# Two ReLUs to VectorE, two weight casts to GpSimd, and a tighter schedule for batch 1 in a fused FFT filter and FFN kernel

## The chip, the cores and the metric

The kernel runs on one core of one Trainium2 chip. The metric is the device time of one execution in microseconds (us). Seven runs of the kernel before gave a median of 795.35 us, from 794.17 to 797.23 us. Besides these, one execution was taken with the hardware profiler; all durations below come from it.

## The reference

The input `x` has 8 batches of 3008 rows with 256 columns. Each batch goes through a filter in the frequency domain along its rows, and all 24064 resulting rows go through a two-layer network with a squared ReLU:

```
X = np.fft.rfft(x, axis=1)
y = np.fft.irfft(X * (filt_r + 1j * filt_i)[None], n=3008, axis=1)
h = np.maximum(y.reshape(24064, 256) @ w_in, 0.0)     # w_in: 256 x 2048
out = h * h @ w_out                                   # w_out: 2048 x 256
```

## The kernel before, in words

**The filter of one batch** is done with matrix products in four stages, because 3008 = 64 x 47. Stage A (`unit_a`, L346) transforms along the 47; its result `u` goes to a scratch tensor `dU` in device memory and is read back in another order as `ut` (`read_u`, L430). Stage B (`unit_b`, L437, twelve units p = 0 to 11) transforms along the 64 into PSUM (`psB`); VectorE multiplies with the filter (L451), makes two half copies (L458, L459) and adds (`unit_s`, L465). Stage P (`unit_p`, L487, twelve units) transforms back into `psP`; ScalarE evacuates it (L496) and every third unit writes to the scratch tensor `dZ` (L499). `read_z` (L508) reads `dZ` back as `zt` (eight DMAs on the SP queue), and stage Y (`unit_y`, L516, sixteen units n = 0 to 15) finishes into `yt`, evacuated by ScalarE for even n (and for n = 12 to 15 of batch 0) and by VectorE for the other odd n (L537, L539).

**The network** runs over 47 groups of 512 rows, each in 8 slots. In slot k of group g, `ffn_g1` (L544) computes two blocks of 128 hidden units into the PSUM tile `psH` (four matmuls of 512 columns, L560) and ScalarE applies the ReLU and writes float16 `h` (L564). `ffn_sq` (L566) squares it on VectorE (L568). One group later `ffn_g2` (L570) multiplies with `w_out` into `psO` (eight matmuls of 256 columns, L577), and `ffn_out` (L580) evacuates `psO` on ScalarE and stores. The first half of a product sums over the `h` of slots 0 to 3 and of the weight rows of cast chunks 0 and 1, the second half over the rest.

**The order is written out by hand**; every engine works off its instructions in the order in which the program issues them. Global slot s issues, in this order: `ffn_g1`; the filter work planned for (s, place 0); `ffn_g2` of the group before; the filter work of (s, place 1); `ffn_out`; `ffn_sq`. `fft_plan(b)` (L608) gives the slots of batch b's filter work. For batch 1, plan slot r is global slot r. So on VectorE the square of slot s stands behind all filter work of slot s. Batch 0's filter is done in a prologue before slot 0, except for its stage Y units 4 to 15, which are planned into slots 4 to 23.

**Buffers** that matter here are rings of two: `psH` (so the product of slot s waits for the ReLU of slot s-2), and `psF`, which stages A, B, P and Y share in order of issue (a unit waits until the tile of two units before is evacuated). `h` has two buffers too; the second group's takes the place of the float32 `w_out` that the four `cast_wout` (L329, 1024 columns each) turn into float16 `sWout`. In slots 0 to 7 there is no `psO` work yet, and slot 8's `psH` needs the four stage Y units of slots 4 to 7.

Of the kernel before, what the change touches and what calls it, by code (L numbers as in the profile page):

```python
# [11 lines left out]
AF = mybir.ActivationFunctionType  # L12
# [98 lines left out]
def kernel(  # L111
# [9 lines left out]
    nc = tc.nc  # L121
# [38 lines left out]
    def psO(name):  # L160
        return pps.tile([128, 2, 256], F32, tag="psO", name=name, bufs=2)

    def psH(name):
        return pps.tile([128, 2, 512], F32, tag="psH", name=name, bufs=2)
# [107 lines left out]
    ps = psO("warm").rearrange("p a d -> p (a d)")  # L272
# [267 lines left out]


    h2s, pso = {}, {}

    def ffn_g1(g, s):  # L544
        if s == 0:
            h2s[g] = p_h2.tile([128, NJT, TG], F16, tag="h2", name=f"h2_{g}")
        h2 = h2s[g]
        ps = psH(f"psH_{g}_{s}")
        segs = []
        t = g * TG  # L550
        while t < (g + 1) * TG:
            b, r = divmod(t, S)
            n = min((g + 1) * TG - t, S - r)
            segs.append((t - g * TG, b, r, n))
            t += n
        for i in range(2):
            jt = 2 * s + i
            for o, b, r, n in segs:
                for dt in range(2):
                    nc.tensor.matmul(ps[:, i, o:o + n],  # L560
                                     sWin[:, dt, jt * 128:(jt + 1) * 128],
                                     yts[b][:, dt, r:r + n],
                                     start=(dt == 0), stop=(dt == 1))
        nc.scalar.activation(out=h2[:, 2 * s:2 * s + 2, :], in_=ps, func=AF.Relu)  # L564

    def ffn_sq(g, s):  # L566
        v = h2s[g][:, 2 * s:2 * s + 2, :]
# [40 lines left out]
    def fft_plan(b):  # L608

        plan = {}  # L610

        def put(r, place, f, *a):
            plan.setdefault((r, place), []).append((f, a))

        if b == 1:
            for n in range(4, 16):
                put(n if n < 8 else n + 2 if n < 12 else 2 * n - 7, n % 2, unit_y, 0, n)
            for k in range(4):
                put((4, 5, 7, 7)[k], 1, cast_wout, k, nc.vector)
        t0 = 2 if b == 1 else 6  # L620
        for a in range(12 if b == 1 else 0, 16):
            put(t0 + a // 2, a % 2, unit_a, b, a)
        put(10 if b == 1 else 14, 1, read_u, b)
        t0 = 14 if b == 1 else 18
        for p in range(12):
            r = t0 + (18 if b == 1 else 19) * p // 11
            put(r, 0, unit_b, b, p)
            put(r, 0, unit_s, b, p)
            put(r + 2, 1, unit_p, b, p)
        t0 = 35 if b == 1 else 40  # L630
        for c in range(4):
            put(t0, 1, read_z, b, c)
        if b + 1 < B:
            for c in range(2):
                put(t0 - 13, 1, load_x, b + 1, c)
            for c in range(4):
                r = t0 - 8 + 3 * c
                put(r, 1, cast_x, b + 1, c)
                if c < 2:
                    put(r, 1, load_x, b + 1, c + 2)  # L640
        for n in range(16):
            if b == 1:
                put(38 + n // 2 if n > 3 else 39, n % 2, unit_y, b, n)
            else:
                put(44 + n // 2, n % 2, unit_y, b, n)
        return plan
# [79 lines left out]
    for b in range(1, B):  # L726
        first = (b * S // TG) * SLOTS - (48 if b > 1 else 40)
        for (r, place), w in fft_plan(b).items():
            work[(first + r, place)] = w

    for s in range((NG + 1) * SLOTS):
        g, k = divmod(s, SLOTS)
        if g < NG:
            ffn_g1(g, k)
        run(work, s, 0)
        if g > 0:
            ffn_g2(g - 1, k)
        run(work, s, 1)
        if g > 0:
            ffn_out(g - 1, k)  # L740
        if g < NG:
            ffn_sq(g, k)
# [30 lines left out]
```

## Time and profile before

| what | value |
|---|---|
| median of seven runs | 795.35 us |
| profiled execution, device time | 797.66 us |
| its span, first to last instruction | 795.8 us |
| granted TensorE clock, mean | 0.997 |
| busy: PE / VectorE (DVE) / ScalarE (ACT) / GpSimd (POOL) | 781.6 / 552.5 / 554.9 / 24.3 us |
| GpSimd's last instruction ends | 43.94 us |
| slot 0's first `psH` matmul starts | 51.65 us |
| slot 8's `psO` matmuls start | 62.81 us |
| VectorE busy, 80 to 100 us and 100 to 120 us | 18.95 and 19.32 us |

The profile page gives the busy time of each engine. The chain of waits follows the last instruction back to what released it, step by step. The timeline lists each engine's instructions with start, duration, source line and, in square brackets, the idle time before it and what ended that. A matmul's printed duration includes its way through the array; four of 512 columns show 1.03 us from the first start to the last end, but the next matmul can start 0.86 us after the first start.

### The profile page before, as it was taken

How to read it: one execution, taken by the hardware profiler on the slowest of the kernel's cores; microseconds unless marked ns; L12 is line 12 of the kernel's file. 1: busy time of each engine (PE TensorE's matmuls, PEld its weight loads, DVE VectorE, ACT ScalarE, POOL GpSimd, SP SyncE). 2: the span in 40 equal slices, each digit the busy share in tenths (PEclk: the TensorE clock that was granted, in tenths of full speed). 3: DMA queues.
4: the chain of work that ended last, by engine and by line, in shares of the span. 5: the costliest groups of instructions: out<-in, count | busy, mean ns of one | idle time of the engine just before them, and what ended most of it. 6: DMA issues, size and time to landing. Idle time of an engine off the chain costs nothing.

```text
span 795.8 us, 14801 instructions
## 1 busy us (share of the span) xinstructions
PE 781.6 (98%) x6102; PEld 553.2 (70%) x6102; DVE 552.5 (69%) x898; ACT 554.9 (70%) x708; POOL 24.3 (3%) x27
## 2 busy tenths in 40 slices
PE   8989999999999999999999999999999999999998
PEld 6746767666676676867777676776767667776666
DVE  6946995579755897559965699557995589554342
ACT  3856776777677677767777677676777767766664
POOL 3710000000000000000000000000000000000000
PEclk9999999999999999999999999999999999999999
DMA  9994555346723567055471555525664342511111
GB/s 352 358 274 140 143 149 133 88 134 163 198 57 107 161 163 180 31 166 151 123 180 51 168 153 136 130 70 156 151 182 89 89 140 80 137 35 41 40 41 54
DMA packets 88139, 107.32 MB, mean 135 GB/s; under 512 B 6288, under 2 KB 78864, under 8 KB 83856
## 3 DMA queue, kind: packets, MB, share of 16 engines
q1 hardware_dynamic: 87864, 106.19, 46.8%
q8 instruction: 48, 0.79, 0.4%
q10 hardware_dynamic: 144, 0.18, 0.1%
q14 instruction: 19, 0.16, 0.1%
q0 software_dynamic: 64, 0.00, 0.0%
HBM read 58.12 MB, written 48.23 MB: 134 GB/s over the span
## 4 chain that ended last, share of the span: by engine, by line
PE 91%; DMA 5%; DVE 2%; ACT 1%; issue 0%; SPq 0%; POOL 0%; ACTq 0%; POOLq 0%
PE psO L577 40%; PE psH L560 38%; PE psA L359 3%; PE psY L530 3%; PE psB L443 2%; PE psP L494 2%; DMA ut<-dU 2%; DMA zt<-dZ 1%; DMA xw<-in_x_dram 1%; PE warm L274 1%; DVE ut L428 1%; ACT h L564 1%; DMA dU<-u 0%; DMA dZ<-ze 0%; PE psf L293 0%; DVE h L568 0%
## 5 line engine op out<-in xcount | busy, mean ns | idle before, releaser
L564 ACT ACTIVATE h<-psH 128x1024 f16<-128x1024 f32 x376 | 385.2, 1025 | 190.6 <-PE psH L560 187.7
L577 PE MATMUL psO<-sWout,h 128*128 128x256 f16 x3008 | 388.7, 272 | 0.0
L560 PE MATMUL psH<-yt,sWin 128*128 128x512 f16 (+7 forms) x1728 | 386.9, 351 | 1.8 <-DVE yt L539 0.8
L577 PEld LDWEIGHTS <-h 128*128 128x128 f16 x3008 | 290.6, 98 | 77.3
L568 DVE TENSOR_TENSOR h<-h 128x1024 f16<-128x1024 f16 x376 | 253.8, 685 | 100.7 <-ACT h L564 99.2
L560 PEld LDWEIGHTS <-sWin 128*128 128x128 f16 x1728 | 159.5, 98 | 101.7 <-issue 3.5
L451 DVE TENSOR_TENSOR prod<-psB,sF 128x1024 f16<-128x1024 f32 x84 | 102.4, 1219 | 6.7 <-PE psB L443 6.5
L539 DVE CAST yt<-psY 128x376 f16<-128x376 f32 x62 | 34.0, 549 | 57.4 <-PE psY L530 57.4
L365 DVE CAST u<-psA 96x512 f16<-96x512 f32 x50 | 34.3, 687 | 47.3 <-PE psA L359 45.1
L496 ACT CAST ze<-psP 128x512 f16<-128x512 f32 x84 | 49.2, 586 | 17.8 <-PE psP L494 15.9
L588 ACT COPY ost<-psO 128x512 f32<-128x512 f32 (+1 forms) x96 | 55.7, 580 | 6.7 <-PE psO L577 5.3
L530 PEld LDWEIGHTS <-zt 112*128 112x128 f16 x512 | 34.9, 98 | 12.0 <-issue 1.6
L530 PE MATMUL psY<-sC,zt 112*128 112x94 f16 x512 | 42.3, 205 | 0.7 <-DMA zt<-dZ 0.4
L465 DVE TENSOR_TENSOR yf<-prod,yf 128x512 f16<-128x512 f16 x84 | 35.7, 425 | 2.9
L443 PE MATMUL psB<-ut,sSB 128*128 128x256 f16 x192 | 36.5, 272 | 1.0 <-DMA ut<-dU 0.8
L359 PE MATMUL psA<-x,sC 94*96 94x512 f16 x96 | 36.6, 382 | 0.0
L443 PEld LDWEIGHTS <-sSB 128*128 128x128 f16 x192 | 18.6, 98 | 21.8 <-issue 2.7
L494 PE MATMUL psP<-yf,sSP 128*128 128x256 f16 x168 | 32.1, 273 | 0.2 <-ACT yt L537 0.2
L537 ACT CAST yt<-psY 128x376 f16<-128x376 f32 x66 | 30.7, 468 | 1.1 <-PE psY L530 0.6
L338 DVE CAST x<-x 94x2048 f16<-94x2048 f32 x24 | 29.2, 1216 | 0.0
L363 ACT CAST u<-psA 96x512 f16<-96x512 f32 x50 | 28.6, 572 | 0.0
L458 DVE COPY yf<-prod 64x512 f16<-64x512 f16 x84 | 24.3, 289 | 2.9
(63 smaller groups left out, 253.2 us busy)
## 6 DMA issues: line engine op xcount, KB each, us to landing
x<-in_x_dram SPq DMA_DIRECT2D x20, 768.0 KB
zt<-dZ SPq DMA_DIRECT2D x64, 192.0 KB
dU<-u SPq DMA_DIRECT2D x28, 384.0 KB
dZ<-ze SPq DMA_DIRECT2D x28, 384.0 KB
out_dram<-ost SPq DMA_DIRECT2D x66, 128.0 KB
out_dram<-ost SPq DMA_DIRECT2D x31, 256.0 KB
ut<-dU SPq DMA_DIRECT2D x7, 1024.0 KB
xw<-in_x_dram SPq DMA_DIRECT2D x4, 1024.0 KB
```

Of the source, the lines that this page charges most:

```text
L359: nc.tensor.matmul(ps[0:96, :], sSA, x16s[(b, c)][:, m, :], start=True, stop=True)
L443: nc.tensor.matmul(ps[:, i * D:(i + 1) * D], sSB[:, 2 * p + i, :], uts[b][:, 2 * p + i, :], start=True, stop=True)
L451: nc.vector.tensor_mul(out=prod, in0=ps.rearrange("p (a d) -> p a d", d=D).unsqueeze(1).to_broadcast([128, 2, 2, D]), in1=sF[:, :, 2 * p:2 ...
L465: nc.vector.tensor_add(out=yf, in0=prod[:, 0], in1=yf)
L494: nc.tensor.matmul(ps[:, i * D:(i + 1) * D], sSP[:, 2 * p + i, :], yf[:, i, :], start=True, stop=True)
L496: nc.scalar.copy(out=zes[(b, c)][:, 2 * i6:2 * i6 + 2, :], in_=ps.rearrange("p (a d) -> p a d", d=D))
L530: nc.tensor.matmul(ps[:, 94 * jj:94 * jj + 94], zt[:, 4 * (g % 2) + jj, dt * 128:(dt + 1) * 128], sSY, start=True, stop=True)
L560: nc.tensor.matmul(ps[:, i, o:o + n], sWin[:, dt, jt * 128:(jt + 1) * 128], yts[b][:, dt, r:r + n], start=(dt == 0), stop=(dt == 1))
L564: nc.scalar.activation(out=h2[:, 2 * s:2 * s + 2, :], in_=ps, func=AF.Relu)
L568: nc.vector.tensor_mul(out=v, in0=v, in1=v)
L577: nc.tensor.matmul(pso[g][:, t % 2, :], h2s[g][:, jt, t * 128:(t + 1) * 128], sWout[:, jt, :], start=(jt == 0), stop=(jt == NJT - 1))
L588: nc.scalar.copy(out=ost[:, h0:h0 + step, :], in_=pso[g][:, h0:h0 + step, :])
```

## The change

Three edits, all of which concern slots 0 to 39, that is the first network groups and batch 1's filter.

1. The ReLUs of slots 2 and 5 of group 0 are done by `nc.vector.tensor_relu` instead of ScalarE's activation.
2. Of the four casts of `w_out`, chunks 0 and 1 go from VectorE to GpSimd (slots 4 and 5 as before). Chunks 2 and 3 stay on VectorE; chunk 2 is issued in slot 6 instead of slot 7, so ahead of slot 7's stage Y unit 7.
3. In batch 1's plan the twelve units of stage B spread over 17 slots instead of 18, and stage P follows two slots later as before; `read_z` goes from slot 35 to 34, the loads of batch 2's `x` from 22 to 21, and its casts from slots 27, 30, 33, 36 to 26, 29, 32, 35 (with the loads that follow the first two).

Unit p of stage B is in these slots:

| p | 0 | 1 | 2 | 3 | 4 | 5 | 6 | 7 | 8 | 9 | 10 | 11 |
|---|---|---|---|---|---|---|---|---|---|---|---|---|
| before | 14 | 15 | 17 | 18 | 20 | 22 | 23 | 25 | 27 | 28 | 30 | 32 |
| after | 14 | 15 | 17 | 18 | 20 | 21 | 23 | 24 | 26 | 27 | 29 | 31 |

```diff
+    on_vector = {(0, 2), (0, 5)}
...
-        nc.scalar.activation(out=h2[:, 2 * s:2 * s + 2, :], in_=ps, func=AF.Relu)
+        if (g, s) in on_vector:
+            nc.vector.tensor_relu(out=h2[:, 2 * s:2 * s + 2, :], in_=ps)
+        else:
+            nc.scalar.activation(out=h2[:, 2 * s:2 * s + 2, :], in_=ps, func=AF.Relu)
...
             for k in range(4):
-                put((4, 5, 7, 7)[k], 1, cast_wout, k, nc.vector)
+                put((4, 5, 6, 7)[k], 1, cast_wout, k, nc.gpsimd if k < 2 else nc.vector)
...
         for p in range(12):
-            r = t0 + (18 if b == 1 else 19) * p // 11
+            r = t0 + (17 if b == 1 else 19) * p // 11
             put(r, 0, unit_b, b, p)
             put(r, 0, unit_s, b, p)
             put(r + 2, 1, unit_p, b, p)
-        t0 = 35 if b == 1 else 40
+        t0 = 34 if b == 1 else 40
```

## The prediction

> **What bounds the kernel now.** I read the page first: it says which engine is full.
>
> ```profile
> PE 781.6 (98%) x6102; PEld 553.2 (70%) x6102; DVE 552.5 (69%) x898; ACT 554.9 (70%) x708; POOL 24.3 (3%) x27
> ```
>
> PE is busy for 98% of the span, and from slot 8 on its matmuls follow each other without a gap for most of the time. So an edit counts only by what it does to PE's gaps. The chain of waits from 50 to 64 us shows the gaps of the first group (start, duration, engine and line):
>
> ```profile
> 52.94 1.03 ACT h L564
> 53.97 0.04 issue
> 54.02 1.04 PE psH L560 x4
> 55.05 0.02 issue
> 55.08 1.95 ACT h L564 x2
> 57.02 0.02 issue
> 57.05 0.69 DVE h L568
> 57.74 0.61 DVE sWout L331
> 58.34 0.61 DVE h L568
> 58.96 0.46 DVE yt L539
> 59.42 0.60 DVE sWout L331
> 60.02 1.20 DVE h L568 x2
> 61.22 0.47 DVE yt L539
> 61.69 0.04 issue
> 61.73 0.81 PE psH L560 x3
> ```
>
> Up to 57.02 ScalarE's ReLUs set the pace, and from 57.05 VectorE does, without a pause, until its evacuation of stage Y unit 7 lets slot 8's second matmul start at 61.73. How much is there to win? Between 54.02 and 62.38 (PE's next other work) PE issues seven `psH` of 0.86 and four stage Y units of 0.17, 6.70 of 8.36 us: 1.66 us of gaps. The same view from 62.5 to 125 us is PE, but for some 0.3 us near 82.5, and then about 0.75 us at slots 39 and 40, where the first stage Y units of batch 1 wait for each other's evacuation.
>
> **ReLUs and casts in the first group.** I walk VectorE's queue with the durations of the chain. The price of a ReLU on VectorE is not in the trace; the nearest rows (mean ns of one after the bar) have its shape, or its size out of SBUF:
>
> ```profile
> L428 DVE CAST ut<-psT 128x1024 f16<-128x1024 f32 x2 | 2.4, 1218 | 1.1 <-PE psT L420 1.1
> L331 DVE CAST sWout<-wout 128x1024 f16<-128x1024 f32 x4 | 2.7, 684 | 0.0
> ```
>
> I take d = 1.22, since the source is PSUM; 0.68 is the low end, and the slowest VectorE row of 1024 columns (L451, 1.219 mean) says that 1.23 is the high end. ScalarE's is 1.02.
>
> - Slot 2: VectorE has the square of slot 1 at 54.91 and is free 0.60 later, at 55.51, although the product is ready at 55.06. ReLU 55.51 to 56.73; on ScalarE it ended at 56.05. The new wait is PE's: slot 4's product waits for this ReLU in the `psH` ring, so it starts at 56.78, not 56.15, and all PE work stands behind it.
> - Slot 4: product ready 1.02 later, at 57.80; ScalarE's ReLU 57.84 to 58.86; square on VectorE at 58.89.
> - Slot 5: ReLU behind that square, 59.50 to 60.72. Slot 7's product waits for it: 60.77 instead of 59.58, a PE gap of 0.83.
> - VectorE goes on: stage Y unit 5 at 60.64 (0.47), square 5 at 61.11 (0.60), cast 2, now here, at 61.71 (0.61), square 6 at 62.32 (0.61), unit 7 at 62.93. Plus 0.47 and 0.04: slot 8's second matmul starts at 63.44 instead of 61.73.
>
> So the two casts that leave save 1.21, but two ReLUs and the earlier cast 2 put 2 x 1.14 + 0.61 in, and the ring wait adds the rest: **+1.71 us**. With d left open, unit 7 starts at 60.49 + 2d against 61.22 before: +0.65 at d = 0.68, and no loss only below 0.36. PE then is gapless, so nothing gives the time back.
>
> Casts 0 and 1 on GpSimd I cost at nothing. GpSimd is empty after 43.94, so nothing is queued behind them. The data were there at 57.74, when VectorE's cast started unheld. GpSimd's casts of 1024 columns take 1.02 to 1.56; two end by 60.9 at the latest, and `psO` of slot 8 needs them at 62.81, or 64.5 in the new order. That cover is 1.9 us; beyond it each late us is a PE us. The low end is 0; the high end is VectorE held by GpSimd's use of the memory, bounded by what one such meeting cost in this row, 1.56 less 1.02, twice: 1.1. I take 0.
>
> ```profile
> 12.06 1.56 POOL L232 CAST xw<-xw 128x1024 f16<-128x1024 f32 x1 [9.39 <-DMA xw<-in_x_dram]
> ```
>
> This row ran beside a VectorE cast (12.03, 0.69, no longer than the others of its kind); later ones took 1.02. It was GpSimd that paid. The Trainium skill, "GPSIMD Engine Reference" (its opening table), speaks against edit 2: GpSimd shares its SBUF interfaces with VectorE, and two-port or two-input VectorE instructions contend; it does not say who pays. By that rule alone the sum could be 1.1 higher, by the row it stays.
>
> **Stages B and P closer together.** "Moved up" is a squeeze: units 0 to 4 stay, units 5 and 7 to 11 come one slot earlier, unit 6 stays; P likewise. VectorE is the tight engine there: 18.95 and 19.32 of 20 us busy. Durations from the timeline, start to start: unit B 2.22 (1.26 + 0.30 + 0.32 + 0.34), square 0.60, cast of x 1.14; a PE slot is 1.73, plus 0.22 for each B or P and 0.17 for a Y. I walk with times as before, without the shift above:
>
> - Up to slot 20 nothing changes; VectorE starts unit 4 (B4) at 88.31. Then: square 20, unit 5 at 91.13, squares 21 and 22, unit 6 at 94.57 (before: 95.21).
> - Slot 23 now holds B6, Y15 and P5. P5 wants the `psF` tile of B6, whose multiply ends at 95.79; PE would be there at 95.40. PE waits **0.43**, with slot 24 behind it.
> - Square 23, B7 97.39, squares 24 and 25 to 100.83, B8 101.23, x cast, square 26, B9, squares 27 and 28, B10 at 108.63, x cast, squares 29 and 30 to 113.21. Now B11 comes in slot 31, ahead of square 31; before it came after it, in slot 32. B11 113.21 to 115.43, square 31 until 116.12.
> - Slot 33's `psO` reads slot 31's `h` with its last two of eight matmuls, 0.65 after its start, that is at 115.38 with the 0.43 included. They wait **0.78**.
>
> The last wait had little slack before (timeline; slots 30 and 31's squares, slot 33's `psO`, B11):
>
> ```profile
> 113.28 1.28 DVE L568 TENSOR_TENSOR h<-h 128x1024 f16<-128x1024 f16 x2
> 114.30 1.04 PE L577 MATMUL psO<-sWout,h 128*128 128x256 f16 x8
> 114.49 1.21 DVE L451 TENSOR_TENSOR prod<-psB,sF 128x1024 f16<-128x1024 f32 x1
> ```
>
> The squares ended at 114.56, needed at 114.95: 0.39 of slack, against 2.22 of B11 put in front, less what comes from the earlier start. Together **+1.21**, from -0.75 (if slots 39 and 40 lost their gap) to +2.2 (a whole unit B). Behind the waiting P5 stand slot 24's `psH` and B7, for which ScalarE and VectorE wait; behind slot 33's `psO` stand P11, its `dZ` write and the `zt` reads.
>
> The DMAs that move are on SP: `dZ` writes, eight `zt` reads, four x loads and, with their odd slots unmoved, the output stores they pass. SP waits in this stage for evacuations (11.9 us for `ze`, 11.7 for the x casts), so order costs nothing there. The `zt` reads were issued from 118.42 to 124.07, and stage Y at 124.94 did not wait for them: to have them earlier gains nothing. An x cast held by a late load would hold square 32 or 35, needed at slots 40 and 41: 8 us and more of cover. GpSimd's queue has nothing else to pass.
>
> **Sum.** 1.71 + 1.21 = 2.92 us on the profiled execution: 797.66 to 800.6, span 798.7. The median stands 2.31 lower than that execution, so I forecast 795.35 + 2.9 = **798.3**, its own range 797.5 to 799.2.
>
> **Rivals.**
> 1. Only the first group costs (19%): VectorE catches up and P5 waits on nothing. 795.35 + 1.7 = 797.1. For it: VectorE idled 0.38 and 0.21 us at 92.39 and 102.55. Against: the 2.22 in front of square 31.
> 2. The faster side (6%): the ReLUs fit into VectorE's idle time and relieve ScalarE, whose ReLUs hold the `psH` ring up to 57. Price: at most the 1.66 us of gaps, 793.7. It decides from d below 0.36; no row of that size is under 0.68.
> 3. TensorE's clock drops (13%). Rows by stretch:
>
> ```profile
> 40.00:43.00 3.00, 0.52 (x4) 0.25 (x3) 0.00 (x0) 1.01 (x1) 1.09 (x2) 1.00 1.01 309
> 44.00:47.00 3.00, 3.00 (x9) 1.41 (x8) 1.38 (x2) 0.48 (x1) 0.00 (x0) 0.50 0.47 134
> ```
>
> PE was busy 0.52 of 3 us, and from 44 to 47 the granted clock was 0.50. In my walk PE works 1.25 of the 3.5 us before 63.44 (gaps 0.83 and 1.43). If that trips it, some 3.3 us at half speed cost 1.7: 800.0. The Trainium skill, "TensorE: Matmul & The Clock Gate" (Part 1), puts the drop after an idle window of about 3.4 us; by that rule my gaps are too short and the sum has no such term.
>
> 4. The change does not act as named (12%): the ReLU runs at the 0.68 end and the squeeze is hidden: 795.35 + 0.65 = 796.0.
>
> **How the numbers follow.** The forecast has 50%. Slower by over 0.2% (1.6 us, about what a measurement tells from no change, so above 796.94): forecast, rival 3 and 0.12 of rival 1: 0.75. Within: rival 4 and 0.07 of rival 1: 0.19. Faster: 0.06. The range reaches from rival 4 (795.9) to rival 3 with a little of the upper bounds (800.6).
>
> **What would show it.** Right: a VectorE row for the ReLU near 1.22 us; PE waiting for VectorE's `h` at slots 4 and 7; slot 8's second matmul near 63.4; P5 waiting for `prod`; slot 33's `psO` waiting for the square. Wrong: a ReLU under 0.7 us, or slot 8 before 61.73; PE gapless from slot 20 to 34; gaps gone at slots 39 and 40.

## The result and the profile after

The changed kernel takes 800.2 us, the median of 16 runs (798.27 to 802.12), against 796.08 us, the median of 40 runs of the kernel before (the seven shown above and later ones). The ratio is 1.0052, with a 95% interval from 1.0042 to 1.0062: slower by 4.1 us, between 3.3 and 4.9. The forecast was slower, by 2.9 us. The profiled execution took 799.73 us; its span is 798.0 us, 2.2 us longer than that of the profiled execution before.

The page's line of busy times hardly moves, because busy time does not show waits:

```profile
PE 780.3 (98%) x6102; PEld 552.5 (69%) x6102; DVE 554.7 (70%) x898; ACT 553.4 (69%) x706; POOL 26.8 (3%) x29
```

In the changed file the VectorE ReLU is line 566, ScalarE's 568 and the square 572; `psH` is 561 and `psO` 581. This is the chain of waits of the first group after the change (start, duration, engine and line), to be laid beside the one from 52.94 us in the prediction:

```profile
51.54 2.83 DVE h L572 x2
54.37 1.15 DVE h L566
55.52 0.04 issue
55.56 1.04 PE psH L561 x4
...
57.68 0.69 DVE h L572
58.37 1.14 DVE h L566
...
60.56 0.60 DVE sWout L331
61.16 0.60 DVE h L572
61.76 0.47 DVE yt L539
62.23 0.04 issue
62.27 0.81 PE psH L561 x3
```

The chain has become VectorE's. Both ReLUs (L566) stand on it, then cast 2 and square 6, and slot 8 waits for the evacuation (L539) as before. But the first line was not in the prediction: the squares of slots 0 and 1 take 2.83 us together, where one took 0.69. At that time GpSimd does its two casts (timelines of GpSimd and VectorE, one instruction a line):

```profile
51.35 1.04 POOL L331 CAST sWout<-wout 128x1024 f16<-128x1024 f32 x1 [8.20 <-DMA wout<-in_moe_w_out_dram]
51.54 1.39 DVE L572 TENSOR_TENSOR h<-h 128x1024 f16<-128x1024 f16 x1 [2.00 <-DMA zt<-dZ]
52.33 1.50 POOL L331 CAST sWout<-wout 128x1024 f16<-128x1024 f32 x1
52.85 1.52 DVE L572 TENSOR_TENSOR h<-h 128x1024 f16<-128x1024 f16 x1
```

The bracket of the first square names a DMA that ended about then; the ReLU that this square needs ended at 51.5 too. The rows look like taking turns: the first cast starts ahead of a square and keeps its usual 1.04 us, and each instruction that starts while the other engine's is under way takes 0.5 to 0.8 us longer. The casts are written in slots 4 and 5, but GpSimd has nothing else in its queue, so they start when `w_out` has landed, at 51.35, beside the squares of slots 0 and 1.

Further on, PE's timeline shows the two waits of stages B and P (in brackets the wait and what ended it):

```profile
96.48 0.38 PE L494 MATMUL psP<-yf,sSP 128*128 128x256 f16 x2 [0.27 <-DVE prod L451]
116.78 0.39 PE L581 MATMUL psO<-sWout,h 128*128 128x256 f16 x2 [0.59 <-DVE h L572]
```

The bracket counts from the modelled end of the matmul before, which overlaps the next; by starts the two waits are 0.43 and 0.75 us.

**Where the 2.2 us of the two spans lie.** I cut the span at first `psH` matmuls; these lengths are used below. G runs from slot 0's first `psH` matmul to slot 8's second, M from slot 14 to slot 35.

| stretch | before | after | difference |
|---|---|---|---|
| start to slot 0 | 51.65 | 49.20 | -2.45 |
| G, slot 0 to slot 8 | 10.08 | 13.07 | +2.99 |
| slot 8 to 14 | 12.63 | 12.63 | 0 |
| M, slot 14 to 35 | 42.76 | 44.07 | +1.31 |
| slot 35 to 41 | 12.55 | 12.54 | -0.01 |
| slot 41 to the end | 666.13 | 666.49 | +0.36 |

G and M together are +4.3, close to the 4.1 of the medians. The -2.45 is not the change's doing, since the change touches nothing ahead of slot 0: in this execution of the kernel before, PE waited 2.48 us for GpSimd's cast of x and the clock was at 0.50 from 44 to 47 us; in this one of the changed kernel it waited 1.73 us and the clock stayed at 1.00. That recurs below.

### The profile page after: what moved, and what is told of

The parts are those of the page before. It is cut to its first block, busy times and chain, and to the rows that moved or that the text cites. A ratio compares the mean times of both kernels' runs of the same rounds, so it can differ in the third digit from the quotient of the medians.

```text
span 798.0 us, 14800 instructions
## 1 busy us (share of the span) xinstructions
PE 780.3 (98%) x6102; PEld 552.5 (69%) x6102; DVE 554.7 (70%) x898; ACT 553.4 (69%) x706; POOL 26.8 (3%) x29
## 4 chain that ended last, share of the span: by engine, by line
PE 89%; DMA 5%; DVE 4%; ACT 1%; issue 0%; SPq 0%; POOL 0%; ACTq 0%; POOLq 0%
PE psO L581 38%; PE psH L561 37%; PE psA L359 3%; PE psY L530 3%; PE psB L443 2%; PE psP L494 2%; DMA ut<-dU 2%; DMA zt<-dZ 1%; DVE h L572 1%; DVE prod L451 1%; PE warm L274 1%; DMA xw<-in_x_dram 1%; PE psf L293 1%; PE psf L296 1%; ACT sF L303 0%; DMA dU<-u 0%
## 5 line engine op out<-in xcount | busy, mean ns | idle before, releaser
L539 DVE CAST yt<-psY 128x376 f16<-128x376 f32 x62 | 34.0, 549 | 58.0 <-PE psY L530 58.0
```

## The experiments

Times are differences of medians to runs of the kernel before on the same chip. The ratio beside them is not that of the two medians, so it can say up to 0.9 us more or less; its 95% interval decides what is a difference.

**One edit at a time.** First edit 1 alone (the diff's first part), then edit 2 alone, edit 3 alone, and edits 1 and 2 together.

> Edit 1 alone: the ReLUs of slots 2 and 5 on VectorE, all four casts on VectorE in slots 4, 5, 7, 7, no squeeze. Two stage lengths tell the theories apart: G, from slot 0's first psH matmul to slot 8's second (10.08 us in the kernel before, 13.07 in the changed one), and M, from slot 14's first psH matmul to slot 35's (42.76 before, 44.07 changed). My theory has three separate prices: the ReLUs behind squares in VectorE's queue (+1.7), squares held by GpSimd's casts in front of the first ReLU (+1.3), the squeeze (+1.2 to 1.3). It expects the squares of slots 0 and 1 to take 0.69 us each, G 11.8, M 42.8, time +1.7 us. Rival: the slow squares come from DMA traffic that lands in the same microseconds, not from GpSimd: squares near 1.4 us here too, G 13.1, time +3.0.

> Edit 2 alone: casts 0 and 1 on GpSimd, cast 2 on VectorE in slot 6. My theory: the squares of slots 0 and 1 are held by GpSimd's casts and take about 2.8 us together where they took 1.4, but with the ReLUs on ScalarE no product waits for VectorE there, and the queue has caught up by slot 5; cast 2 in slot 6 stands ahead of stage Y unit 7. G 10.2, M 42.8, time +0.1 us (no difference that can be measured). Rival, that the casts on GpSimd are what costs by themselves: G 11.4, time +1.3. Rival, that DMA traffic slows the squares: squares as in the kernel before, 0.69 us each, or slow in the run with edit 1 alone too.

> Edit 3 alone: stages B and P of batch 1 over 17 slots, reads of dZ and the x loads and casts one slot earlier. My theory: G 10.08 as before; P5 waits 0.43 for the multiply of B6, slot 33's last two psO matmuls wait 0.75 for the square of slot 31; M 44.0, time +1.2 us. Rival: the waits of this stage in the changed kernel are carried over from the late first group, and the squeeze alone costs nothing: M 42.8, time as before.

> Edits 1 and 2 without the squeeze. My theory: the price of the ReLUs and that of the held squares meet, since slot 2's ReLU now stands behind the held squares: G 13.1, M 42.8, time +3.0 us. Rival, that the two edits only add up (edit 1 +1.7, edit 2 near nothing): G 11.8, time +1.7.

| run | time | ratio, interval | G | M |
|---|---|---|---|---|
| edit 1 alone | +2.0 | 1.0030 (1.0013 to 1.0047) | 11.85 | 42.77 |
| edit 2 alone | -0.4 | 1.0004 (0.9987 to 1.0020) | 10.32 | 42.81 |
| edit 3 alone | +1.5 | 1.0022 (1.0008 to 1.0037) | 10.08 | 43.96 |
| edits 1 and 2 | +1.7 | 1.0026 (1.0010 to 1.0042) | 12.57 | 42.77 |

Edit 1 alone, VectorE's timeline around slot 2's ReLU:

```profile
55.19 0.69 DVE L572 TENSOR_TENSOR h<-h 128x1024 f16<-128x1024 f16 x1 [2.00 <-ACT h L568]
56.10 0.69 DVE L572 TENSOR_TENSOR h<-h 128x1024 f16<-128x1024 f16 x1 [0.22 <-ACT h L568]
56.71 1.22 DVE L566 TENSOR_SCALAR h<-psH 128x1024 f16<-128x1024 f32 x1
```

The squares take 0.69 us, the ReLU 1.22 and follows the square: G grows by 1.77, with GpSimd out of it. The walk gave 1.71 for edits 1 and 2 together; it holds here too, since cast 0 falls into VectorE's idle time ahead of square 4 and cast 1 stands where the walk has cast 2. Edit 3 alone has both its waits and M +1.20, without the late first group: nothing is carried over.

Edit 2 alone was not what I expected in one respect: its squares were at 0.69 us. In that execution slot 0 began at 52.70 and GpSimd's casts ran from 52.35 to 54.38, before the first square at 55.05; they did not meet. In the run with edits 1 and 2 slot 0 began at 49.22, the casts ran from 50.86 to 53.34 and the squares from 51.57, at 2.32 together: they met, and G is 0.72 longer than with edit 1 alone. In the changed kernel they met more, and it is 1.22 longer. The expectation for edits 1 and 2 (G 13.1, time +3.0) was too high; the time, +1.7, is what its rival had, and G, 12.57, is between the two. So the third price depends on when slot 0 starts against a transfer that lands at its own time.

**Does GpSimd hold VectorE, and which instructions?** One run lets GpSimd start behind slot 1's square, with edits 1 and 2:

```
     def ffn_sq(g, s):
...
+        if (g, s) == (0, 1):
+            nc.gpsimd.tensor_copy(out=gate, in_=h2s[0][0:1, 3, 511:512])
```

> Edits 1 and 2 as in the run before, but GpSimd first copies one element of slot 1's square, so its two casts start only when that square is done; no squeeze. In that run, G (slot 0's first psH matmul to slot 8's second) was 12.57 us, with the squares of slots 0 and 1 at 2.32 us together beside GpSimd's casts; with edit 1 alone 11.85 and 1.38. My theory: what GpSimd's cast holds is a VectorE instruction with two inputs in SBUF; the ReLU reads PSUM and stays at 1.21 us, and the squares of slots 2 and 3, held now, have 0.84 us of slack ahead of slot 4's square. Squares of slots 0 and 1 at 0.69 each, G 11.9 to 12.1, time +1.8 to +2.0 us against the kernel before. Rival: GpSimd holds any VectorE instruction, the ReLU too: ReLU of slot 2 near 2 us, G 12.6 or more.

G was 11.85, as with edit 1 alone and as the walk had it for both edits. The time, +0.6, is less than the +1.8 to +2.0 expected, though the interval (ratio 1.0015, 1.0001 to 1.0028, so up to 2.2 us) does not exclude that. The timeline of VectorE and GpSimd (slot 2's ReLU, the next three squares, GpSimd's casts):

```profile
54.74 1.21 DVE L567 TENSOR_SCALAR h<-psH 128x1024 f16<-128x1024 f32 x1
55.99 2.83 DVE L573 TENSOR_TENSOR h<-h 128x1024 f16<-128x1024 f16 x3
55.01 2.01 POOL L331 CAST sWout<-wout 128x1024 f16<-128x1024 f32 x2
```

The ReLU reads PSUM and runs at its 1.21 us beside a cast. The three squares take 2.83 instead of about 1.9, since one of them meets the second cast, and there nobody waits for it. The other run measures the price by itself, in the kernel before:

```
+    scrap = p_prod.tile([128, 2, 2, D], F16, tag="prod", name="scrap").rearrange("p a b d -> p (a b) d")
...
+    for _ in range(8):
+        nc.gpsimd.tensor_copy(out=scrap, in_=w32s[2][:, 0:4, :])
     prologue[0] = False
```

> The kernel before with eight extra GpSimd casts of 128x1024 float32 to float16 out of the loaded w_out, into a tile that nobody reads, from when the data land on; nothing else is changed, and the output is the same. This measures by itself what VectorE loses beside GpSimd's casts. My theory: VectorE's squares (two inputs in SBUF) and its casts out of SBUF that meet them go from 0.69 us to about 1.4, the evacuations out of PSUM stay at 0.54; VectorE's queue sets slot 8, so G goes from 10.08 to 12.5 to 14.5 us; GpSimd's casts go from 1.02 to 1.2 to 1.6 each; time +2.5 to +4.5. Rival: GpSimd alone pays, squares stay at 0.69, G 10.1, time as before.

Groups by line and shape from 53.5 to 64.5 us of that run (busy, mean ns of one after the bar):

```profile
L723 POOL CAST scrap<-wout 128x1024 f16<-128x1024 f32 x8 | 10.9, 1357 | 9.3 <-DMA wout<-in_moe_w_out_dram 8.9
L569 DVE TENSOR_TENSOR h<-h 128x1024 f16<-128x1024 f16 x7 | 9.3, 1346 | 2.2 <-ACT h L565 2.2
L331 DVE CAST sWout<-wout 128x1024 f16<-128x1024 f32 x2 | 2.6, 1294 | 0.0
L539 DVE CAST yt<-psY 128x376 f16<-128x376 f32 x1 | 0.5, 535 | 0.0
```

A line of PE's timeline, slot 8's second matmul, and the stretch 66 to 69 us of the same run (PE's busy time after the length, the granted clock third from the end):

```profile
65.78 0.59 PE L561 MATMUL psH<-yt,sWin 128*128 128x512 f16 x1 [3.78 <-DVE yt L539]
66.00:69.00 3.00, 3.00 (x11) 1.49 (x10) 1.53 (x3) 1.37 (x2) 0.00 (x0) 0.50 0.01 3
```

Squares go from 690 to 1346 ns (the mean of seven, the first of which started ahead of GpSimd and took 693), VectorE's casts out of SBUF from 684 to 1294, the evacuation from PSUM stays (542 before, 535 here), GpSimd's casts go from 1.02 to 1.36 us. G is 15.05, more than the 12.5 to 14.5 that I expected, and the time +5.0 us, ratio 1.0066 (1.0047 to 1.0085), from four runs. The time is not the price of the meeting alone: behind PE's wait of 3.78 us the clock was at 0.50 until 70 us, and slots 8 to 14 took 14.69 instead of 12.63 us. Both engines pay. The theory stands, its rival (GpSimd alone pays) falls.

**Are stages B and P just full?** Edit 3 alone, without its two meetings:

```
-                put(n if n < 8 else n + 2 if n < 12 else 2 * n - 7, n % 2, unit_y, 0, n)
+                put(n if n < 8 else n + 2 if n < 12 else 2 * n - 7 - (n == 15), n % 2, unit_y, 0, n)
...
+            r = t0 + (17 if b == 1 else 19) * p // 11 + (b == 1 and p == 11)
```

> Edit 3 alone, with its two meetings taken out: stage Y unit 15 of batch 0 goes from slot 23 to 22, so that P5's psF tile is not the one that B6 has just filled, and B11 (with P11) stays in slot 32, behind slot 31's square, as in the kernel before. Edit 3 alone had M, from slot 14's first psH matmul to slot 35's, at 43.96 us against 42.76. My theory: the loss is these two waits and nothing else: M 42.8, time as before. Rival: VectorE is simply full in this stage, and the same work in fewer slots loses its time somewhere else: M 43.5 or more, time +0.7 or more.

M was 42.77, neither wait is there, and the time is -0.4 us, ratio 0.9992 (0.9980 to 1.0004). The squeeze costs its two waits and nothing else.

**A better order.** VectorE's queue in front of stage Y unit 7 sets the first group. So:

```
-                put(n if n < 8 else n + 2 if n < 12 else 2 * n - 7, n % 2, unit_y, 0, n)
+                put(n - 1 if n < 8 else n + 2 if n < 12 else 2 * n - 7, n % 2, unit_y, 0, n)
...
-                put((4, 5, 7, 7)[k], 1, cast_wout, k, nc.vector)
+                put((4, 6, 7, 7)[k], 1, cast_wout, k, nc.vector)
...
-                put(38 + n // 2 if n > 3 else 39, n % 2, unit_y, b, n)
+                put(38 + n // 2, n % 2, unit_y, b, n)
```

> None of the three edits. Instead stage Y units 4 to 7 of batch 0 go one slot earlier (3 to 6), the casts of w_out stay on VectorE in slots 4, 6, 7, 7 (cast 1 behind unit 7), and the first two stage Y units of batch 1 go from slot 39 to 38. My theory of the first group, that VectorE's queue ahead of unit 7 sets slot 8's second matmul: unit 7 now stands ahead of square 6 and of three casts, so the next bound is ScalarE's ReLU of slot 6 near 60.8 on the clock of the kernel before: G 9.1 to 9.3 us (10.08 before). The gap of about 0.75 us at slots 39 and 40 closes. Time -1.6 us. Rival: ScalarE sets the first group anyway: G 9.9 or more; and the reads of dZ have not landed by slot 38, so PE waits for DMA there as long as it waited for evacuations.

G was 9.18, as expected, and slot 8 waits for ScalarE's ReLU, no more for VectorE. Slots 35 to 41 took 12.71 instead of 12.55: there the rival was right, PE waited 0.69 us for the reads of `dZ` in slot 38. Time -1.8 us, ratio 0.9982 (0.9969 to 0.9995). That it meets the -1.6 expected is in part chance: the stretches from slot 0 to 41 add up to -0.7, and sorted by the clock as below, against runs on the same chip, the mean falls by 0.8 and 1.1.

**The clock ahead of slot 0.** Eight matmuls on zeros fill PE's wait for GpSimd's cast of x:

```
+    ps = psO("warm2").rearrange("p a d -> p (a d)")
+    for _ in range(8):
+        nc.tensor.matmul(ps, zero, sF[:, 0, 0:2, :], start=True, stop=True)
     for c in (0, 2, 1):
         chunk_a(1, c)
```

> The kernel before with eight extra matmuls of 128x512 on zeros, into a PSUM tile that nobody reads, in the prologue just ahead of batch 1's stage A, where PE waits 1.7 to 2.5 us for GpSimd's cast of x. The profiles so far fall into two sorts: slot 0's first psH matmul at 48.97 to 50.87 us where the granted clock stayed near 1.00 from 43 us on, or at 51.37 to 52.84 where it was near 0.5 for some 3 to 5 us after that wait. My theory: PE's idle time there trips the clock in a part of the executions, and that, not the kernels' edits, makes most of the spread of single runs. With the idle time filled, slot 0 starts at 50 us or before and the clock stays at 1.00 from 43 to 48; the median falls by 1 to 2.5 us and the runs lie within 3 us. Rival: the extra matmuls do not fit into the wait, and the clock drops for another reason: slot 0 at 51 us or later, time as before or up to 1.7 us longer.

The stretches 40 to 43 and 43 to 48 us of that run; the first number after the length is PE's busy time, the third from the end the granted clock:

```profile
40.00:43.00 3.00, 2.94 (x16) 1.46 (x14) 0.00 (x0) 1.32 (x2) 1.81 (x2) 1.00 0.91 275
43.00:48.00 5.00, 4.90 (x28) 2.74 (x27) 3.27 (x5) 2.87 (x6) 0.21 (x1) 1.00 0.74 200
```

Slot 0 began at 49.27. The 12 runs lie from 795.34 to 797.09, those of the kernel before beside them from 794.42 to 800.29. In all 12 the mean clock was 0.999 or 1.000. The median fell by 0.6 only, ratio 0.9994 (0.9980 to 1.0007), no sure difference. My expectation was right on the clock and the spread and too high on the median: in executions that kept the clock anyway the mean is higher with the matmuls, 796.01 against 795.41 over all comparisons and 794.96 on the same chip. The two sorts of profiles in the expectation were not clean: the run that lets GpSimd start later had slot 0 at 50.87 and yet a clock of 0.50 from 43.1 to 46.4.

**Two combinations that failed.** The first joins the early units, a squeeze whose four x casts wait until slots 32, 34, 36 and 38, and the early units of slot 38; the second adds the eight matmuls.

```
-                r = t0 - 8 + 3 * c
+                r = 32 + 2 * c if b == 1 else t0 - 8 + 3 * c
```

> What the runs so far point to, without ReLUs on VectorE and without casts on GpSimd: stage Y units 4 to 7 of batch 0 one slot earlier and cast 1 behind unit 7 (this alone gave G 9.18); the squeeze of edit 3 with unit B11 in slot 31, but unit 15 of stage Y in slot 22, and the four x casts of batch 2 in slots 32, 34, 36, 38, behind B11, instead of 26, 29, 32, 35; and batch 1's first two stage Y units in slot 38, for which the reads of dZ now start a slot earlier. My theory: G 9.2; M (slot 14's to slot 35's first psH matmul) 42.8, since slot 31's square has 2.28 us less in front of it; slot 35's to slot 41's 11.8 (12.55 before, 12.71 with the early units alone, which waited 0.69 for DMA). Time -1.6 us. Rival: the reads of dZ still land too late, or slot 31's square still holds slot 33: 35 to 41 at 12.4 or more, M 43.3 or more, time -0.5 to -0.9.

> The two runs before together: the rearranged order and the eight extra matmuls ahead of batch 1's stage A. My theory: the two gains add, since one lies before slot 0 and the other behind it: time -2.5 to -4 us. Rival, that an earlier slot 0 meets reads that have not landed (stage Y unit 4, now in slot 3, needs the second zt tile): PE waits for DMA in slots 3 to 6, and the sum is no better than the rearranged order alone.

Both were slower, by 8.4 us (ratio 1.0117, 1.0091 to 1.0144) and 9.6 us (1.0116, 1.0089 to 1.0142). In the first, M was 42.77: with the x casts behind B11 and unit 15 in slot 22 the squeeze is free. Most of the loss is one wait. SP's, VectorE's and PE's timelines (issues of the `zt` reads and of the last x load; the last x cast; slot 40's `psH`):

```profile
113.69 7.82 SPq L512 DMA_DIRECT2D zt<-dZ  x8
121.61 0.37 SPq L192 DMA_DIRECT2D x<-in_x_dram  x1
130.36 1.22 DVE L338 CAST x<-x 94x2048 f16<-94x2048 f32 x1 [9.94 <-DMA x<-in_x_dram]
133.15 1.07 PE L560 MATMUL psH<-yt,sWin 128*128 128x64 f16 x5 [7.09 <-DVE yt L539]
```

The last x load stood on SP behind the reads of `dZ`, which waited for `dZ`'s writes. Its cast, planned in slot 38 all the same, held VectorE's queue for 9.94 us, with the evacuations that slot 40 needs behind it, and PE waited 7.09 us. Slots 35 to 41 took 22.20 instead of 12.55 us; in them are also 1.24 us of waiting for the reads of `dZ` at slot 38, which the rival had, and a clock of 0.50 from 131 to 137 us, around the end of the long wait. The long wait was my own mistake in the order, and neither theory had it.

The last run keeps only the early units and the eight matmuls:

> What is left of the rearranged order after its long wait: only stage Y units 4 to 7 of batch 0 one slot earlier with cast 1 behind unit 7, and the eight extra matmuls ahead of batch 1's stage A. Nothing of the squeeze, of the x casts or of slots 38 to 40 is touched. My theory: G 9.2 us, M and slots 35 to 41 as in the kernel before (42.76 and 12.55), slot 0 near 49.3 with the clock at 1.00; the two gains add, -0.9 and -0.6: time -1.5 us, and runs within 3 us of each other. Rival: with slot 0 early, unit 4 (now slot 3) waits for the second zt tile: G 9.8 or more, time -0.6 or less.

G was 9.18, M 42.77, slots 35 to 41 12.54, slot 0 at 49.45, all as expected. But the time was -0.1 us, ratio 0.9995 (0.9981 to 1.0009). The 0.9 us of the first group do not come out in the median; beside the run with the eight matmuls alone, PE's waits for `ut` were 0.9 instead of 0.5 us, which accounts for less than half. The stretch from slot 41 to the end, the same code in all kernels, took from 665.2 to 667.9 us in the profiled executions, which is more than the gain that was looked for. Whether an order beats both kernels by more than noise is left open; the run with the early units in the order above beats the changed kernel surely and the kernel before by a little (its interval ends at 0.9995).

**The clock sorts the runs.** Each run has its mean granted clock. I split at 0.999; the 98 runs of the kernel before are pooled over all these comparisons, on four chips. Mean time in us, number of runs and the difference to the kernel before of the same sort:

| kernel | clock 0.999 and above | below |
|---|---|---|
| before | 795.41 (43) | 797.58 (55) |
| changed | 799.64 (7), +4.2 | 800.87 (9), +3.3 |
| edit 1 | 797.07 (5), +1.7 | 800.04 (7), +2.5 |
| edit 2 | 795.80 (6), +0.4 | 797.88 (6), +0.3 |
| edits 1 and 2 | 797.87 (6), +2.5 | 799.37 (6), +1.8 |
| edits 1 and 2, GpSimd later | 796.62 (6), +1.2 | 798.92 (6), +1.3 |
| edit 3 | 796.53 (2), +1.1 | 798.76 (10), +1.2 |

The run with edits 1 and 2 loses 2.5 us where the clock stays and 1.8 where it drops. That fits casts that are over before the squares begin when slot 0 is late, as in the profile of edit 2 alone: from the stage lengths one gets 2.49 (casts met) and 1.77 (not met). The changed kernel should lose the squeeze's 1.2 more: 4.2 with the G of its own profile, and 3.0 where the casts do not meet. Edit 2 alone loses next to nothing in both sorts, which suggests that the held squares cost time only together with the ReLUs; no profile shows edit 2 alone with casts that met. The groups are small, and edit 1's two differences ought to be equal, so this is support and no proof.

## Why the prediction was right, and where it was wrong

- **ReLUs in VectorE's queue, +1.71:** right. Edit 1 alone gave G +1.77, the ReLU 1.21 to 1.22 us for the 1.22 taken, and PE's waits stood at slots 4 and 7 and at slot 8's second matmul. The later GpSimd start gave 11.85 with edits 1 and 2, the walk's own order. (A slip without weight: by the prediction's own 60.49 + 2d the low end d = 0.68 gives +0.63, not +0.65.)
- **Casts 0 and 1 on GpSimd at nothing:** this is the step that failed. The prediction read off one row that "it was GpSimd that paid" and took 0 of a range up to 1.1. VectorE's squares pay as well, 1346 instead of 690 ns while they meet. In the changed kernel that is 1.22 us (G 13.07 less 11.85), just beyond the range's upper end, because slot 2's ReLU stands behind the held squares. The row was read rightly but shows one case only: there VectorE's cast started 0.03 us ahead (12.03 against 12.06) and GpSimd paid; in the changed kernel GpSimd's cast starts ahead (51.35 against 51.54) and the square pays. Nor did the prediction ask when the casts would run: it took their data as there at 57.74, but they ran from 51.35 to 53.83, as soon as `w_out` landed. The cover named for the casts, until `psO` of slot 8, was right and did not matter: what they cost is on VectorE, not their own lateness.
- **The squeeze, +1.21:** right in both places, 0.43 at P5 and 0.75 at slot 33, and M +1.20 alone. That earlier `zt` reads gain nothing was right too: slots 39 and 40 keep their gap.
- **An x cast held by a late load has 8 us of cover:** nothing in the changed kernel speaks against it, its slots 35 to 41 took 12.54 us. In the first failed combination, with the casts later and the last load behind the reads of `dZ`, one cast waited 9.94 us and PE 7.09: more than that cover.
- **Rivals:** the clock did not drop in the first group (1.00 from 50 to 66 us, though PE waited 2.06 us ahead of slot 4 and was busy 1.70 of 3 us from 60 to 63), as the page's rule had it. So rival 3 did not occur, though its 800.0 is nearest to the measured 800.2: that is chance. Rival 1 falls with M, +1.31, and rivals 2 and 4 with a ReLU of 1.21 to 1.22 us. The drop before slot 0, which rival 3 took its price from, is not in every execution: 55 of 98 runs of the kernel before had a mean clock below 0.999.

With the held squares the sum is 1.71 + 1.22 + 1.21 = 4.1, the measured difference; the forecast fell short by that one term. That it fits so well is in part luck: the 1.22 comes from one execution (0.72 in the run with edits 1 and 2), and the changed kernel loses 4.2 us where the clock stays and 3.3 where it drops. The median of 800.2 us also lies above the forecast's own range, 797.5 to 799.2, and 0.7 of that is that the kernel before has a median of 796.08 over 40 runs, not 795.35.

## What to carry to other kernels

Before work goes to an engine because it has time, look where it stands in that engine's queue and who waits behind it: two ReLUs that each take 0.2 us longer than on ScalarE cost 1.8 us, because they stood behind squares and ahead of products. Ask also when it will run: an engine with an empty queue starts when its data land, wherever the program writes the work. A cast given to GpSimd does not leave VectorE free while VectorE works out of SBUF; where VectorE is the bound, give GpSimd its work when VectorE idles or evacuates PSUM. When units of a stage are drawn together, list for each buffer and each group boundary what now falls into the same slot: the whole price were two such meetings, and moving two units took them away.

## What the runs showed of the hardware

VectorE and GpSimd slow each other while both work out of SBUF: squares of 1024 columns 1346 instead of 690 ns, casts 1294 instead of 684, GpSimd's casts 1.36 instead of 1.02 us; instructions that read PSUM were not slowed (the ReLU 1.21 us, an evacuation 0.54). In the first pair of each meeting the one that started ahead kept its time and the other paid: VectorE's cast at 12.03 against GpSimd's at 12.06 us (the kernel before), GpSimd's cast at 51.35 against the square at 51.54 us (the changed kernel). It shows as longer busy time, not as a wait. The Trainium skill, "GPSIMD Engine Reference" (its opening table), names the contention with two-port or two-input VectorE instructions; the runs agree and show that both engines pay.

The granted clock can drop to 0.50 around PE's wait for GpSimd's cast of x in the prologue. Of the eleven profiled executions without the eight matmuls, whose code ahead of slot 0 is the same, it dropped, for 3.3 to 6.9 us, in the five where that wait was 1.81 to 2.48 us, and not in the six where it was 0.91 to 1.73 us. More than half of the runs of the kernel before (55 of 98) have a mean clock below 0.999, and they take 2.2 us longer, the longer wait included. With the wait filled by matmuls, none of 24 runs had a mean clock below 0.999; the five runs of the second failed combination, which have these matmuls too, had 0.995 or 0.996, from a drop at the end of its long wait, 131 to 137 us. The length of one wait is not all that counts: 2.06 us ahead of slot 4 in the changed kernel left the clock at 1.00.

The Trainium skill, "TensorE: Matmul & The Clock Gate" (Part 1), has the activity window run freely, not in step with the kernel. With that agrees that the drop came at different moments, from 1.2 us before the end of the wait (edit 2 alone) to 1.0 us after it (the kernel before). But the wait itself differs between executions, and no run here tells the two apart. By the idle window of about 3.4 us that the prediction took from the page all these waits would be too short; the measurement decides.
